# Windowed attention and a mixture of four domains on one core: the bias table is folded earlier, half of the next head pair's q is prepared ahead, and the mask reads SBUF

## The chip, the cores and the metric

The kernel runs on one core of a Trainium2 chip. The metric is device microseconds of one execution, the median of the runs; smaller is better. TensorE (PE in the profile) multiplies matrices, VectorE (DVE), ScalarE (ACT) and GpSimd (POOL) work on elements, SyncE (SP) and ACT issue the transfers of this kernel. Matmuls write to PSUM, which is handed out in banks; all else lies in SBUF.

## The reference

Two parts in a row. First attention in a window, with a bias that grows with the distance between query and key, by a slope for each head:

```
B, H, S, D = 4, 8, 768, 64;  n_global, n_local = 8, 96
scores = q @ k.T / sqrt(D)
rel = pos[:, None] - pos[None, :]
is_global = pos[None, :] < n_global
is_local = (rel >= 0) & (rel < n_local)
dist = where(is_global & ~is_local, n_local, abs(rel))
scores = where(is_global | is_local, scores - slopes[:, None, None] * dist, -1e9)
a = softmax(scores);  x = (a @ v) as [B * S, H * D] = [3072, 512]
```

Then a mixture of E = 4 domains with F = 1024 hidden columns, weighted by the normalised probabilities p of each row:

```
out = sum over e of p[:, e:e+1] * (relu(x @ w1[e]) @ w2[e])
```

## The kernel before

The mixture's products are the bulk of the work. Each float32 operand is split into a rounded high part and a rest, so that a product takes three matmuls (high·high, high·rest, rest·high). The product with w1 is built block by block from seven products of sums of blocks in place of eight (`first`; blocks are called B11, T1 and so on, their epilogues write p, u, vv and h), the one with w2 follows in `second`, and DVE adds it to `acc` by domain.

The kernel runs in three stages. Until about 62 us `attention_early` computes batch 0's attention alone, in the order of the program, with steps that a counter n numbers; `chores` (loads and splits of weights) are woven between, and the step `opening` starts the mixture. Then come batches 0 and 1 of the mixture, one `first` or `second` after the other, each in steps. Between the steps the generator `attention_chain` is advanced, which does the attention of batches 1, 3 and 2, four pairs of heads each, twelve pairs: `count` steps of it over the length `span`. In this stage (from step 14 on, `HELDSTEPS`) the tile scheduler, not the program, sets the order on each engine: it puts an instruction where its model finds it ready, and hands out PSUM slots as they come free. From about 650 us on `late_batch` runs batches 3 and 2 of the mixture with no attention beside.

A pair takes twelve steps before. Three prepare it: half 0 of q (`prepare_q`: three transposes by TensorE into a bank of the pool pt, a scaled copy by ACT and the rest by DVE into qd), half 0 of k (`prepare_k`, the same into kd), half 1 of q. Then six tiles of 128 queries (t = 0 to 5), with one step more before t = 1 (half 1 of k), t = 2 (loads of the next q and k) and t = 3 (`differences` of v). `spread_q` copies qd to the other 64 partitions by transfers that ACT issues, since each head is used with both halves of the partitions. Each step calls `flow`, a pipeline of four tiles: scores of the newest into ps; `softmax` of the next (DVE reads ps and nbias, ACT takes exp into pb with the sum zsum) and the normalising of the one before (ACT scales pb into pn); `turn_folded` transposes pn into a bank of pt and moves it to pT; after the sixth tile `weigh` multiplies pT with v and vg in two halves, each into a bank of pt, which ACT copies to x (batches 1 and 2) or `piece` (batch 3).

A tile sees 96 older keys, its own 128, and 32 global ones. They are folded to 160 columns: an old key and the one that can't be seen at the same place share a column, and `newer` is the mask that tells them apart. For this `nbias`, the table of biases by head, is folded too, and `attention_chain` does so at its first call:

```
ve.tensor_tensor(nbias[:, :, :NPREV], nbias[:, :, :NPREV], nbias[:, :, PL : 2 * P], op=ALU.min)
for to, fro, n in (
    (PL, 2 * P + NGLOB, NPREV), (2 * P + NGLOB, NPREV, NGLOB), (NPREV, P, NGLOB), (P, 2 * P + NGLOB, NGLOB),
):
    ve.tensor_copy(nbias[:, :, to : to + n], nbias[:, :, fro : fro + n])
```

`ve`, `ac`, `po`, `te` and `sy` are the five engines behind a helper; all that goes through it has the helper's line, L43, in the profile, so work is told apart by the names of its tiles.

Of the kernel before, what the change touches and what calls it, by code (L numbers as in the profile page):

```python
# [14 lines left out]
ALU = mybir.AluOpType  # L15
# [3 lines left out]
P = 128  # L19
NEG = 1.0e9  # L20

NGLOB = 32
NPREV = 96
# [163 lines left out]
def attn_moe_kernel(ctx: ExitStack, tc, q, k, v, n_global, n_local, domain_probs, w1, w2, out):  # L187
# [4 lines left out]
    NQT = S // P  # L192
# [246 lines left out]
    def softmax(A, new, old):  # L439


        if old:
            pb, zsum = old["pb"], old["zsum"]
        if new:
            t, pr, ps = new["t"], new["pr"], new["ps"]
            if A.early:
                width = 2 * P
                cols = slice(0, P) if t == 0 else slice(0, width)
                bcol = slice(2 * P, 3 * P) if t == 0 else slice(0, width)
                new["pcol"] = pcol = slice(P, width) if t == 0 else slice(0, width)  # L450
            else:
                width = PL
                cols = slice(NPREV, NPREV + P) if t == 0 else slice(0, width)
                bcol = slice(PL, PL + P) if t == 0 else slice(0, width)
                new["pcol"] = pcol = slice(0, P) if t == 0 else slice(0, width)
                if t:
                    both = new["both"]
                    mask = newer[:, P + NGLOB - NPREV - 1 : P + NGLOB - 1].bitcast(mybir.dt.uint16)
                    ve.copy_predicated(
                        both[:, :, :NPREV], mask[:, None, :].to_broadcast([P, 2, NPREV]), both[:, :, PL:]  # L460
                    )
            nmax = A.small.tile([P, 2], F32, name="nmax")
            new["zsum"] = A.small.tile([P, 2], F32, name="zsum")
            new["pb"] = A.pb.tile([P, 2, width], F32, name="pb")
        for j in range(2):
            if new:
                e = new["pb"][:, j, pcol]
                ve.tensor_tensor_reduce(
                    e, ps[j][:, cols], nbias[:, 2 * pr + j, bcol], 1.0, 3.0e38, ALU.add, ALU.min, nmax[:, j : j + 1]
                )  # L470
                ac.activation(
                    e, e, AF.Exp, bias=nmax[:, j : j + 1], scale=-1.0, accum_out=new["zsum"][:, j : j + 1]
                )
            if old:
                if j == 1:
                    ve.reciprocal(zsum, zsum)
                elif A.early:

                    old["spare"] = spare = A.small.tile([P, 3], F32, name="spare")
                    ve.tensor_scalar(zsum, zsum, 1e-9, None, op0=ALU.add, op1=ALU.add, accum_out=spare[:, 2:3])  # L480
                else:
                    ac.activation(zsum, zsum, AF.Copy, bias=1e-9)
        if old:
            if A.early:
                for j in range(2):
                    p = pb[:, j, old["pcol"]]
                    ve.tensor_scalar(
                        p, p, zsum[:, j : j + 1], None, op0=ALU.mult, op1=ALU.add, accum_out=old["spare"][:, j : j + 1]
                    )
                return  # L490

            old["pn"] = pn = A.pb.tile([P, 2 * PL], F32, name="pn")
            if old["t"]:
                pieces = ((0, pn[:, :PL], pb[:, 0]), (1, pn[:, PL : PL + NGLOB], pb[:, 1, P:]))
            else:
                pieces = ((0, pn[:, :P], pb[:, 0, :P]),)
            for j, dst, src in (*pieces, (1, pn[:, PL + NGLOB :], pb[:, 1, :P])):
                ac.activation(dst, src, AF.Copy, scale=zsum[:, j : j + 1])

    def turn(A, tile_):  # L500
# [11 lines left out]
    def turn_folded(A, tile_):  # L512

        t, pn = tile_["t"], tile_["pn"]
        pt = A.pt.tile([P, 4, P], F32, name="pt")
        pT = tile_["pT"] = A.pT.tile([P, 2, 2, P], F32, name="pT")
        for place, at in enumerate((0, PL + NGLOB, P)[: 3 if t else 2]):
            te.transpose(pt[:, place, :], pn[:, at : at + P], ident)
        if t:
            ve.scalar_tensor_tensor(  # L520
                pT[:NPREV, 0], newer[:NPREV, None, :P].to_broadcast([NPREV, 2, P]), 1.0, pt[:NPREV, :2],
                op0=ALU.subtract, op1=ALU.mult,
            )
            for j in range(2):
                ac.copy(pT[NPREV:, 0, j], pt[j * NGLOB : (j + 1) * NGLOB, 2])
        ac.copy(pT[:, 1], pt[:, :2])

    def weigh(A, three, x, b):

# [25 lines left out]
    def attention_early(A):  # L555
# [66 lines left out]
        while any(tiles):  # L622
            flow()
            yield

    def attention_chain(bs, A):

        tiles, turned = [None] * 4, []
        order = [(b, pr) for b in bs for pr in PAIRS]
        nats, gots = [{} for _ in order], [{} for _ in order]  # L630

        def flow(new=None):

            one, two, three, four = tiles
            if new:
                new["both"] = scores(A, new["t"], gots[new["m"]])
                new["ps"] = [new["both"][:, j] for j in range(2)]
            if four:
                turned.append(four)
            if len(turned) == NQT:  # L640
                b = order[four["m"]][0]
                for half in (turned[:TPH], turned[TPH:]):
                    weigh(A, half, xs[b], b)
                turned.clear()
            if three:
                turn_folded(A, three)
            softmax(A, one, two)
            tiles[:] = [new, one, two, three]

        def fetch_heads(m, names):  # L650
# [6 lines left out]
        po.iota(  # L657
            newer, pattern=[[1, P + NGLOB]], base=1 - NGLOB, channel_multiplier=-1, allow_small_or_imprecise_dtypes=True
        )
        po.tensor_scalar(newer, newer, 0.0, 1.0, op0=ALU.is_gt, op1=ALU.mult)  # L660
        ve.tensor_tensor(nbias[:, :, :NPREV], nbias[:, :, :NPREV], nbias[:, :, PL : 2 * P], op=ALU.min)
        for to, fro, n in (
            (PL, 2 * P + NGLOB, NPREV), (2 * P + NGLOB, NPREV, NGLOB), (NPREV, P, NGLOB), (P, 2 * P + NGLOB, NGLOB),
        ):
            ve.tensor_copy(nbias[:, :, to : to + n], nbias[:, :, fro : fro + n])
        yield
        for m, (b, pr) in enumerate(order):
            if pr == PAIRS[0]:
                xs[b] = None if b == B - 1 else xp.tile([P, NPAIR, S], F32, name="x")
                if b == B - 1:  # L670
                    xd[b] = dp.tile([P, NPAIR, S], F32, name="x_last")
            nat, got = nats[m], gots[m]
            for part, hf in ((prepare_q, 0), (prepare_k, 0), (prepare_q, 1)):
                part(A, nat[part.__name__[-1]], hf, got)
                flow()
                if part is prepare_k:
                    spread_q(0, got)
                yield
            for t in range(NQT):
                if t in (1, 2, 3):  # L680
                    if t == 1:
                        prepare_k(A, nat["k"], 1, got)
                    elif t == 2:
                        fetch_heads(m + 1, "qk")
                    else:
                        nat["vg"] = differences(A, nat["v"])
                    flow()
                    yield
                flow({"t": t, "pr": pr, "m": m, "v": nat})
# [350 lines left out]
    with ExitStack() as start_stack:  # L1040
        A = Pools(start_stack, "start", st=1, kd=2, qd=2, nat=2, natv=3, pb=4, ps=2, pt=3, px=1, early=True)
        for n, _ in enumerate(attention_early(A)):
            if n == 9:
                chores += [load_plain(2), load_w2(0, lead=5, eng=po)]
            if n == 2 * NQT + 5:
                chores += [load_w1(1, lead=2, hold=0, eng=po), first_sums(0)]
            work_chores()
            if n == 4 * NQT + 1:
                opening(A)
        mix = mixture()  # L1050
        next(mix)
    Ordered.on = False
# [470 lines left out]
```

## Time and profile before

| | us |
|---|---|
| median of 3 runs | 1164.09 (1163.98 to 1166.28) |
| the profiled execution | 1165.77 |
| its span, first to last instruction | 1164.0 |
| TensorE busy | 1137.0 |
| DVE busy | 882.2 |
| ACT busy | 630.8 |
| POOL busy | 625.8 |

The span is the time between the first and the last instruction; the profiled execution's own time is 1.77 us longer. Busy time is the union of an engine's instructions. All durations below are from this one execution.

### The profile page before, as it was taken

To read this page: it belongs to the slowest core of one execution; us is meant where nothing else is said; L and a number is where in the kernel's file an instruction comes from. 1 tells how busy PE (TensorE), PEld (TensorE's weight loads), DVE (VectorE), ACT (ScalarE), POOL (GpSimd) and SP (SyncE) were. 2 spreads that over 40 slices of the span, in tenths; PEclk is the share of its full clock that TensorE was granted. 3 is DMA by queue.
4 is the path that set the end of the run, shared out by engine and by line. 5 is a ranking of instruction groups with operands and counts; after the bars stand their busy time and mean duration, and the time that the engine had idled before them with its cause. 6 is when DMAs were issued, how large, how long until landed. Compare 5 with 4: busy or idle time off the path is not lost.

```text
span 1164.0 us, 21323 instructions
## 1 busy us (share of the span) xinstructions
PE 1137.0 (98%) x7414; PEld 1056.0 (91%) x7414; DVE 882.2 (76%) x2069; ACT 630.8 (54%) x1777; POOL 625.8 (54%) x606
## 2 busy tenths in 40 slices
PE   7899999999999999999999999999999999999997
PEld 5678898988898989889898899999999999999997
DVE  7978778777878777787777777777777777777776
ACT  6844777877753665665675334444444444444443
POOL 5667656555453234322222427777778855555554
PEclk9999999999999999999999999999999999999999
DMA  9547989787776888987968668888887687676763
GB/s 183 150 141 277 300 216 305 246 258 198 288 245 227 277 264 264 272 245 241 278 187 277 212 217 301 307 301 301 287 314 280 244 296 249 241 258 227 258 228 132
DMA packets 180978, 290.80 MB, mean 250 GB/s; under 512 B 86784, under 2 KB 137472, under 8 KB 168576
## 3 DMA queue, kind: packets, MB, share of 16 engines
q1 hardware_dynamic: 172992, 273.63, 71.6%
q10 hardware_dynamic: 7872, 15.74, 4.7%
q8 instruction: 61, 1.00, 0.4%
q14 instruction: 53, 0.43, 0.1%
HBM read 207.93 MB, written 70.78 MB: 239 GB/s over the span
## 4 chain that ended last, share of the span: by engine, by line
PE 86%; POOL 4%; DVE 4%; DMA 2%; ACT 2%; issue 2%; ACTq 0%; POOLq 0%; DVEq 0%
PE pm L43 36%; PE pf L43 19%; PE X L43 11%; PE Y L43 9%; PE pt L43 7%; PE ps L43 3%; POOL w1s L43 1%; DMA qd<-qd 1%; DVE pb L43 1%; POOL sums L43 1%; PE px L43 1%; POOL xT L43 1%; POOL xB L43 1%; POOL w2s L43 1%; DMA raw<-in_moe_w_dram 1%
## 5 line engine op out<-in xcount | busy, mean ns | idle before, releaser
L43 PE MATMUL pm<-w2s,h 128*128 128x512 f32 x1152 | 284.6, 396 | 2.6 <-DVE h L43 1.6
L43 PEld LDWEIGHTS pm<-w2s,h 128*128 128x128 f32 x1152 | 210.6, 188 | 45.9 <-DVE h L43 3.8
L43 ACT ACTIVATE hf<-pf 128x384 f32<-128x384 f32 x128 | 62.8, 492 | 248.3 <-DVE pf L43 247.1
L43 POOL TENSOR_TENSOR hS<-sf,hS 128x384 fp32r<-128x384 f32 x126 | 134.2, 1084 | 112.4 <-ACT hS L43 111.6
L43 DVE SCALAR_TENSOR_TENSOR acc<-pm,prob,acc 128x512 f32<-128x512 f32 x180 | 132.6, 747 | 34.1 <-PE pm L43 31.7
L43 PE MATMUL pm<-xT,w1s 128*128 128x384 f32 x744 | 148.7, 341 | 0.0
L43 PE MATMUL pf<-xT,w1s 128*128 128x384 f32 x768 | 146.5, 335 | 0.9 <-ACT hf L43 0.7
L43 POOL TENSOR_TENSOR sums<-raw 128x256 f32<-128x256 f32 x54 | 38.8, 737 | 183.3 <-DMA raw<-in_moe_w_dram 91.2
L43 PEld LDWEIGHTS pf<-xT,w1s 128*128 128x128 f32 x768 | 131.4, 188 | 1.7 <-ACT hf L43 1.2
L43 PEld LDWEIGHTS pm<-xT,w1s 128*128 128x128 f32 x744 | 127.7, 188 | 0.8 <-issue 0.7
L43 DVE TENSOR_TENSOR hA<-hf,hA 128x384 fp32r<-128x384 f32 x94 | 84.6, 926 | 50.6 <-ACT hA L43 50.6
L43 PE MATMUL pm<-xB,w1s 128*128 128x384 f32 x574 | 118.4, 345 | 2.5 <-DVE h L43 2.4
L43 ACT ACTIVATE pb<-pb,nmax 128x160 f32<-128x160 f32 (+2 forms) x192 | 84.4, 447 | 48.9 <-DVE nmax L43 44.6
L43 PE MATMUL pf<-xB,w1s 128*128 128x384 f32 x576 | 110.7, 335 | 0.2 <-ACT hf L43 0.2
L43 PEld LDWEIGHTS pm<-xB,w1s 128*128 128x128 f32 x574 | 99.4, 188 | 8.2 <-DVE h L43 2.8
L43 ACT ACTIVATE h<-pm 128x384 fp32r<-128x384 f32 x128 | 62.2, 491 | 70.0 <-DVE pm L43 66.5
L43 PEld LDWEIGHTS pf<-xB,w1s 128*128 128x128 f32 x576 | 98.7, 188 | 0.5 <-ACT hf L43 0.4
L43 POOL TENSOR_TENSOR sf<-hf 128x384 f32<-128x384 f32 x63 | 70.4, 1117 | 43.6 <-ACT hf L43 43.6
L43 ACT COPY pT<-pt 128x256 f32<-128x256 f32 (+2 forms) x216 | 71.1, 329 | 21.7 <-DVE pT L43 12.7
L43 DVE SCALAR_TENSOR_TENSOR h<-pm,h 128x384 fp32r<-128x384 f32 x128 | 69.6, 551 | 10.6 <-ACT h L43 9.1
L43 PE MATMUL Y<-w2b,hS 128*128 128x256 f32 x576 | 74.0, 282 | 0.0
L43 PE MATMUL X<-w2b,hS 128*128 128x256 f32 x576 | 73.9, 282 | 0.0
(168 smaller groups left out, 2250.7 us busy)
## 6 DMA issues: line engine op xcount, KB each, us to landing
w1s<-kept SPq DMA_DIRECT2D x47, 1792.0 KB, 8.0
w2b<-kept SPq DMA_DIRECT2D x224, 256.0 KB, 4.2
kept<-w1s SPq DMA_DIRECT2D x16, 1792.0 KB, 7.7
raw<-in_moe_w_dram SPq DMA_DIRECT2D x43, 512.0 KB, 5.2
kept<-w2s SPq DMA_DIRECT2D x16, 1024.0 KB, 9.2
w2s<-kept SPq DMA_DIRECT2D x16, 1024.0 KB, 6.2
qd<-qd ACTq DMA_DIRECT2D x48, 192.0 KB, 4.3
q<-in_q_dram SPq DMA_DIRECT2D x30, 192.0 KB, 5.1
```

The lines of the kernel that those rows point to most:

```text
L43: ins = fn(*args, **kwargs)
```

## The change

It has four parts. The fold of nbias and the making of `newer` become a function, `fold_biases`, called in step 26 of the first attention, the one after `opening`. It has three copies in place of four, on POOL, because the first tile of a sequence (t = 0) now reads its own keys and their biases in their natural order; in exchange its pn is put together from four pieces. In `turn_folded` the masked product comes after ACT's copy and reads that copy in SBUF, not the bank of PSUM. A pair takes eleven steps: half 0 of q is prepared ahead of the fifth tile (t = 4) of the pair before, the extra step before t = 2 loads this pair's v, the one before t = 3 goes, `differences` comes after t = 4, and the next q and k are loaded after t = 1 and t = 3. `count` follows, 138 for 149 steps.

```diff
@@ softmax
-                cols = slice(NPREV, NPREV + P) if t == 0 else slice(0, width)
-                bcol = slice(PL, PL + P) if t == 0 else slice(0, width)
+                cols = slice(2 * NGLOB, 2 * NGLOB + P) if t == 0 else slice(0, width)
+                bcol = slice(2 * P, 3 * P) if t == 0 else slice(0, width)
...
             else:
-                pieces = ((0, pn[:, :P], pb[:, 0, :P]),)
-            for j, dst, src in (*pieces, (1, pn[:, PL + NGLOB :], pb[:, 1, :P])):
+                pieces = [
+                    (j, pn[:, j * (PL + NGLOB) + to : j * (PL + NGLOB) + to + n], pb[:, j, fro : fro + n])
+                    for j in range(2) for to, fro, n in ((0, NGLOB, NPREV), (NPREV, 0, NGLOB))
+                ]
+            for j, dst, src in pieces:
                 ac.activation(dst, src, AF.Copy, scale=zsum[:, j : j + 1])
@@ turn_folded
         if t:
-            ve.scalar_tensor_tensor(
-                pT[:NPREV, 0], newer[:NPREV, None, :P].to_broadcast([NPREV, 2, P]), 1.0, pt[:NPREV, :2],
-                op0=ALU.subtract, op1=ALU.mult,
-            )
             for j in range(2):
                 ac.copy(pT[NPREV:, 0, j], pt[j * NGLOB : (j + 1) * NGLOB, 2])
         ac.copy(pT[:, 1], pt[:, :2])
+        if t:
+            ve.scalar_tensor_tensor(
+                pT[:NPREV, 0], newer[:NPREV, None, :P].to_broadcast([NPREV, 2, P]), 1.0, pT[:NPREV, 1],
+                op0=ALU.subtract, op1=ALU.mult,
+            )
@@ new function, called at n == 4 * NQT + 2
+    def fold_biases():
+        po.iota(
+            newer, pattern=[[1, P + NGLOB]], base=1 - NGLOB, channel_multiplier=-1, allow_small_or_imprecise_dtypes=True
+        )
+        po.tensor_scalar(newer, newer, 0.0, 1.0, op0=ALU.is_gt, op1=ALU.mult)
+        ve.tensor_tensor(nbias[:, :, :NPREV], nbias[:, :, :NPREV], nbias[:, :, PL : 2 * P], op=ALU.min)
+        for to, fro in ((PL, NPREV), (NPREV, P), (P, PL)):
+            po.tensor_copy(nbias[:, :, to : to + NGLOB], nbias[:, :, fro : fro + NGLOB])
@@ attention_chain
-            for part, hf in ((prepare_q, 0), (prepare_k, 0), (prepare_q, 1)):
+            for part, hf in ((prepare_k, 0), (prepare_q, 1)):
...
             for t in range(NQT):
-                if t in (1, 2, 3):
-                    if t == 1:
-                        prepare_k(A, nat["k"], 1, got)
-                    elif t == 2:
-                        fetch_heads(m + 1, "qk")
-                    else:
-                        nat["vg"] = differences(A, nat["v"])
+                if t == 1:
+                    prepare_k(A, nat["k"], 1, got)
+                if t == 4 and m + 1 < len(order):
+                    prepare_q(A, nats[m + 1]["q"], 0, gots[m + 1])
+                if t in (1, 2, 4):
                     flow()
+                    if t == 2 and m:
+                        fetch_heads(m, "v")
                     yield
                 flow({"t": t, "pr": pr, "m": m, "v": nat})
                 if t == 0:
                     spread_q(1, got)
-                if t == 0 and m:
-                    fetch_heads(m, "v")
+                elif t == 1:
+                    fetch_heads(m + 1, "q")
+                elif t == 3:
+                    fetch_heads(m + 1, "k")
+                elif t == 4:
+                    if m + 1 < len(order):
+                        spread_q(0, gots[m + 1])
+                    nat["vg"] = differences(A, nat["v"])
                 yield
@@ the loop over the mixture's steps
-    count, span = 3 * NPAIR * (6 + NQT) + 5, (LATE * 13 * per - 12) * 0.97
+    count, span = 3 * NPAIR * (5 + NQT) + 6, (LATE * 13 * per - 12) * 0.97
```

How the instructions move is shown at three places. The first is DVE in the first steps of the mixture, where one product's epilogue writes u, vv, pm and h. Before, the fold stands among them:

```order
L43 TENSOR_TENSOR u<-pm,p_1187 128x384
L43 TENSOR_TENSOR nbias<-nbias 128x8x96
L43 TENSOR_TENSOR vv<-pm,u 128x384
L43 COPY nbias<-nbias 128x8x96
L43 COPY nbias<-nbias 128x8x32
L43 TENSOR_TENSOR u<-pm,u 128x384
L43 COPY nbias<-nbias 128x8x32
L43 TENSOR_TENSOR pm<-pm,vv 128x384
L43 COPY nbias<-nbias 128x8x32
L43 TENSOR_TENSOR pm<-pm,p_1187 128x384
L43 SCALAR_TENSOR_TENSOR h<-pm,h 128x384
```

Of the change, on the same engine at the same product:

```order
L43 TENSOR_TENSOR u<-pm,p_1193 128x384
L43 TENSOR_TENSOR vv<-pm,u 128x384
L43 TENSOR_TENSOR u<-pm,u 128x384
L43 TENSOR_TENSOR pm<-pm,vv 128x384
L43 TENSOR_TENSOR pm<-pm,p_1193 128x384
L43 SCALAR_TENSOR_TENSOR h<-pm,h 128x384
```

The fold's copies stand on POOL now, between the split of the first units' w1 (w1s) and that of w2 (w2s), at the end of the first attention:

```order
L43 CAST w1s<-sums 128x512
L43 TENSOR_TENSOR w1s<-sums,w1s 128x512
L43 IOTA newer 128x160
L43 TENSOR_SCALAR newer<-newer 128x160
L43 COPY nbias<-nbias 128x8x32 x3
L43 CAST w2s<-raw_1057 128x512
```

So five instructions leave DVE's epilogues, and five, the mask's two among them, come ahead of a split on POOL; the minimum on DVE moves to the same step.

The second place is TensorE where the tenth pair is weighed, ahead of the eleventh pair's half 1 of k: matmuls with v and vg are the weighing (the first half is ten of them, the second twelve), those with ident are transposes, pm is a product of the mixture. Before, from the first half's last four on:

```order
L43 MATMUL pt<-pT,v 64x128 x2
L43 MATMUL pt<-pT,vg 64x128 x2
L43 MATMUL pt<-pT,v 64x128 x2
L43 MATMUL pt<-pT,vg 64x128 x2
L43 MATMUL pt<-pT,v 64x128 x2
L43 MATMUL pt<-pT,vg 64x128 x2
L43 MATMUL pt<-pT,v 64x128 x2
L43 MATMUL pt<-pT,vg 64x128 x2
L43 MATMUL pm<-xB_4563,w1s 128x384 x6
L43 MATMUL pm<-xT_4625,w1s 128x384 x6
L43 MATMUL pt<-ident,k 128x128 x3
```

Of the change, from the transposes of k on; the second half begins behind the five matmuls on xB_4569, and its first matmul waits there for ACT:

```order
L43 MATMUL pt<-ident,k 128x128 x3
L43 MATMUL pt<-pT,v 64x128 x4
L43 MATMUL pt<-pT,vg 64x128 x2
L43 MATMUL pt<-pT,v 64x128 x2
L43 MATMUL pt<-pT,vg 64x128 x2
L43 MATMUL pm<-xB_4569,w1s 128x384 x5
L43 MATMUL pt<-pT,v 64x128 x2
L43 MATMUL pt<-pT,vg 64x128 x2
L43 MATMUL pt<-pT,v 64x128 x2
L43 MATMUL pt<-pT,vg 64x128 x2
L43 MATMUL pt<-pT,v 64x128 x2
L43 MATMUL pt<-pT,vg 64x128 x2
```

The transposes of k, which came two products behind the weighing, come just ahead of it, and five matmuls of a product stand between its halves. ACT at the same place, before:

```order
L43 COPY x<-pt 128x384 x2
L43 ACTIVATE pb,zsum<-pb,nmax 128x128 x2
L43 ACTIVATE zsum<-zsum 128x2
L43 ACTIVATE h<-pm 128x384
L43 ACTIVATE pn<-pb,zsum 128x128 x2
L43 CAST kd<-pt 64x3x128
L43 ACTIVATE h<-pm 128x384
L43 CAST kd<-pt 64x3x128
```

And of the change:

```order
L43 CAST kd<-pt 64x3x128
L43 ACTIVATE h<-pm 128x384 x2
L43 CAST kd<-pt 64x3x128
L43 COPY x<-pt 128x384
L43 ACTIVATE pn<-pb,zsum 128x96
L43 ACTIVATE pn<-pb,zsum 128x32
L43 ACTIVATE pn<-pb,zsum 128x96
L43 ACTIVATE pn<-pb,zsum 128x32
L43 COPY x<-pt 128x384
```

The copy of the first half, which led, now stands behind two casts for kd and two of h. In 11 of the 12 pairs the weighing is split like this: in six of them with a product's matmuls on xB in the gap, in five with four or five matmuls against w2s there and, on ACT, a cast of weights or an exp in the place of the two h.

The third place is TensorE ahead of a pair's first tile. Before, from the transposes of half 0 of q:

```order
L43 MATMUL pt<-ident,q 128x128 x3
L43 MATMUL pt<-ident,pn 128x128 x3
L43 MATMUL pm<-w2s,h 128x512 x12
L43 MATMUL pt<-ident,k 128x128 x3
L43 MATMUL pm<-xB_4561,w1s 128x384 x2
L43 MATMUL pt<-ident,pn 128x128
L43 MATMUL pm<-xB_4561,w1s 128x384 x2
L43 MATMUL pt<-ident,pn 128x128 x2
L43 MATMUL pm<-xB_4561,w1s 128x384 x2
L43 MATMUL pm<-xT_4579,w1s 128x384 x6
L43 MATMUL pm<-xT_4591,w1s 128x384 x2
```

Of the change:

```order
L43 MATMUL pt<-ident,q 128x128 x3
L43 MATMUL pm<-xB_4619,w1s 128x384 x6
L43 MATMUL pm<-xB_4569,w1s 128x384 x6
L43 MATMUL ps<-kd,qd 128x256 x4
L43 MATMUL pt<-ident,pn 128x128 x3
L43 MATMUL pm<-xT_4631,w1s 128x384 x6
L43 MATMUL pm<-w2s,h 128x512 x6
L43 MATMUL ps<-kd,qd 128x256 x4
L43 MATMUL pt<-ident,pn 128x128 x3
L43 MATMUL pm<-w2s,h 128x512 x18
L43 MATMUL pt<-ident,k 128x128 x3
L43 MATMUL pm<-w2s,h 128x512 x12
```

The pair's first scores follow 36 matmuls of the mixture behind the transposes of q before, and 66 behind them in the change: the two tiles of scores shown still belong to the pair before. Behind the transposes of k there are 24 of them in both.

## Rows read from the trace of the kernel before

**Rows 1.** The page's busy time of each engine.
```profile
PE 1137.0 (98%) x7414; PEld 1056.0 (91%) x7414; DVE 882.2 (76%) x2069; ACT 630.8 (54%) x1777; POOL 625.8 (54%) x606
```

**Rows 2.** Busy time by stage (the columns are named in the first line).
```profile
core 0: us, PE busy (x) PEld busy (x) DVE busy (x) ACT busy (x) POOL busy (x), PEclk, DMA share, GB/s
...
62.00:100.00 38.00, 34.33 (x156) 27.74 (x157) 33.15 (x58) 16.74 (x32) 32.42 (x29) 1.00 0.64 208
100.00:650.00 550.00, 544.13 (x3343) 490.52 (x3342) 427.32 (x1071) 355.87 (x1101) 229.85 (x221) 1.00 0.80 252
```

**Rows 3.** TensorE's waits, 62 to 100 us: in total, times, longest.
```profile
PE pm L43 <- DVE h L43: 3.1, 2, 2.4
```

**Rows 4.** DVE's timeline at 82 to 91 us: start, duration, work.
```profile
82.97 1.12 DVE L43 TENSOR_TENSOR nbias<-nbias 128x768 bf16<-128x768 bf16 x1
...
84.48 2.21 DVE L43 COPY nbias<-nbias 128x768 bf16<-128x768 bf16 x2
...
87.08 0.28 DVE L43 COPY nbias<-nbias 128x256 bf16<-128x256 bf16 x1
...
87.75 1.29 DVE L43 COPY nbias<-nbias 128x256 bf16<-128x256 bf16 x1
```

**Rows 5.** TensorE's timeline there; in brackets the wait before.
```profile
90.03 1.15 PE L43 MATMUL pm<-xB,w1s 128*128 128x384 f32 x5 [2.43 <-DVE h L43]
```

**Rows 6.** POOL's timeline, 56 to 68 us.
```profile
67.08 1.86 POOL L43 TENSOR_TENSOR xT<-xB,xT 128x768 fp32r<-128x768 f32 x1 [11.05 <-ACT xT L43]
```

**Rows 7.** DVE's timeline, 57.5 to 63 us.
```profile
62.28 0.56 DVE L43 TENSOR_TENSOR xB<-x 128x384 f32<-128x384 f32 x1 [4.78 <-ACT x L43]
```

**Rows 8.** TensorE's waits, 100 to 650 us, the first four lines.
```profile
PE ps L43 <- DMA qd<-qd: 1.6, 2, 1.2
PE pt L43 <- ACT pn L43: 1.3, 1, 1.3
PE pm L43 <- DVE h L43: 1.0, 2, 0.6
PE pt L43 <- ACT pT L43: 0.8, 1, 0.8
```

**Rows 9.** TensorE's timeline around one wait for qd, and qd's transfers.
```profile
512.75 0.49 PE L43 MATMUL pt<-ident,q 128*128 128x128 f32 x3
...
523.46 0.50 PE L43 MATMUL ps<-kd,qd 128*128 128x256 f32 x2 [1.19 <-DMA qd<-qd]
...
DMA to landing us min/median/max: 2.5/4.3/8.2
```

**Rows 10.** Timelines of ACT and TensorE at the first pair's first pn.
```profile
123.38 0.69 ACT L43 ACTIVATE pn<-pb,zsum 128x128 f32<-128x128 f32 x2
124.77 0.62 ACT L43 CAST w1s<-sums 128x512 fp32r<-128x512 f32 x1 [0.70 <-POOL sums L43]
...
123.83 0.62 PE L43 MATMUL pt<-ident,pn 128*128 128x128 f32 x2 [1.26 <-ACT pn L43]
124.20 1.64 PE L43 MATMUL pm<-w2s,h 128*128 128x512 f32 x6
```

**Rows 11.** Timelines of TensorE and ACT at one weighing.
```profile
524.59 0.66 PE L43 MATMUL pt<-pT,v 128*64 128x128 f32 x8
...
527.14 1.68 PE L43 MATMUL pm<-xB,w1s 128*128 128x384 f32 x8
528.66 0.49 PE L43 MATMUL pt<-ident,k 128*128 128x128 f32 x3
...
529.18 0.47 ACT L43 CAST kd<-pt 64x384 fp32r<-64x384 f32 x1 [0.20 <-PE pt L43]
529.56 0.48 ACT L43 ACTIVATE h<-pm 128x384 fp32r<-128x384 f32 x1
```

**Rows 12.** DVE's groups by form, 100 to 650 us, and the page's group of hA.
```profile
L43 DVE SCALAR_TENSOR_TENSOR pT<-newer,pt 96x256 f32<-96x256 bf16 x60 | 24.6, 410 | 5.4 <-PE pt L43 5.3
...
L43 DVE TENSOR_TENSOR pm<-pm,vv 128x384 f32<-128x384 f32 x56 | 31.3, 558 | 6.5 <-PE pm L43 6.5
...
L43 DVE TENSOR_TENSOR hA<-hf,hA 128x384 fp32r<-128x384 f32 x94 | 84.6, 926 | 50.6 <-ACT hA L43 50.6
```

More of the change, by code (lines that the diff above doesn't have):

```diff
@@ L493, in softmax @@
             if old["t"]:
-                pieces = ((0, pn[:, :PL], pb[:, 0]), (1, pn[:, PL : PL + NGLOB], pb[:, 1, P:]))
-            else:
-                pieces = ((0, pn[:, :P], pb[:, 0, :P]),)
-            for j, dst, src in (*pieces, (1, pn[:, PL + NGLOB :], pb[:, 1, :P])):
+                pieces = (
+                    (0, pn[:, :PL], pb[:, 0]), (1, pn[:, PL : PL + NGLOB], pb[:, 1, P:]),
+                    (1, pn[:, PL + NGLOB :], pb[:, 1, :P]),
+                )
+            else:
+                pieces = [
[3 more added lines that the diff above has]
+            for j, dst, src in pieces:
                 ac.activation(dst, src, AF.Copy, scale=zsum[:, j : j + 1])
@@ L624, in attention_early @@
             yield
+    def fold_biases():
+        po.iota(
+            newer, pattern=[[1, P + NGLOB]], base=1 - NGLOB, channel_multiplier=-1, allow_small_or_imprecise_dtypes=True
+        )
+        po.tensor_scalar(newer, newer, 0.0, 1.0, op0=ALU.is_gt, op1=ALU.mult)
+        ve.tensor_tensor(nbias[:, :, :NPREV], nbias[:, :, :NPREV], nbias[:, :, PL : 2 * P], op=ALU.min)
+        for to, fro in ((PL, NPREV), (NPREV, P), (P, PL)):
+            po.tensor_copy(nbias[:, :, to : to + NGLOB], nbias[:, :, fro : fro + NGLOB])
     def attention_chain(bs, A):
@@ L656, in attention_chain @@
         fetch_heads(0, "qkv")
[L657 to L665, printed above, removed]
         yield
+        prepare_q(A, nats[0]["q"], 0, gots[0])
+        flow()
+        yield
+        spread_q(0, gots[0])
         for m, (b, pr) in enumerate(order):
@@ L672, in attention_chain @@
             nat, got = nats[m], gots[m]
-            for part, hf in ((prepare_q, 0), (prepare_k, 0), (prepare_q, 1)):
+            for part, hf in ((prepare_k, 0), (prepare_q, 1)):
                 part(A, nat[part.__name__[-1]], hf, got)
                 flow()
-                if part is prepare_k:
-                    spread_q(0, got)
                 yield
             for t in range(NQT):
-                if t in (1, 2, 3):
-                    if t == 1:
-                        prepare_k(A, nat["k"], 1, got)
-                    elif t == 2:
-                        fetch_heads(m + 1, "qk")
-                    else:
-                        nat["vg"] = differences(A, nat["v"])
+                if t == 1:
[3 more added lines that the diff above has]
+                if t in (1, 2, 4):
                     flow()
+                    if t == 2 and m:
+                        fetch_heads(m, "v")
                     yield
@@ L1049, in attn_moe_kernel @@
                 opening(A)
+            if n == 4 * NQT + 2:
+                fold_biases()
         mix = mixture()
```

## The prediction

> **What bounds the kernel now.** I read four views, from coarse to fine. The page's list of busy times comes first [rows 1]: TensorE is busy 1137.0 of 1164.0 us, so 27 us is all that any reordering can win. The table of busy times by stage [rows 2] says where the part lies that this change can reach: 3.67 us in 62 to 100 us (the mixture's first steps, no attention yet), and 5.87 us in 100 to 650 us (twelve head pairs woven into the mixture). The granted clock is 1.00 in both, so a microsecond of wait removed is one won. Then I read TensorE's waits in the two stages, for what each waits on [rows 3, 8], and followed the large ones into the timelines. The reader should see that of the 3.67 us 2.43 is a single stop [rows 5], and that of the 5.87 us 4.7 are six waits of at most 1.3 us [rows 8]. TensorE's own work does not change: the same matmuls and transposes are issued.
>
> **The fold of the biases.** Before, DVE runs one minimum and four copies on nbias among the epilogues of a product: 1.12 + 2.21 + 0.28 + 1.29 = 4.90 us [rows 4]. TensorE stops right behind them, 2.43 us at 90.03, for DVE's h [rows 5]. Taking 4.90 us out of a queue that was 2.43 us late leaves some 2.4 us to spare: −2.43. The other 0.7 us of waits for h in that stage (3.1 less 2.4, [rows 3]) has another place and stays.
> What is added lies at the end of the first attention. POOL gets three copies of 8x32 columns beside the mask's two instructions, which are shorter than such a copy (160 columns for 256). No row has this copy on POOL; DVE's rows of it bound it, 0.28 and 1.29 us [rows 4]. So POOL needs 1.4 to 6.5 us. It stands idle for the 11.05 us before 67.08 [rows 6], from 56.03 on, so it is done by 62.5 and the instruction at 67.08, which waits for ACT, does not move. DVE's minimum, 1.12 us, falls in the 4.78 us idle before 62.28 [rows 7]. I cost both at nothing; without that cover the first product would start up to 1.1 us later for DVE, and up to 6.5 for POOL.
> The other order of keys for t = 0 gives ACT four pieces of pn for two, 24 more instructions over twelve pairs, at no more than 0.35 us each (0.69 for two, [rows 10]): 8 us at most. ACT has 194 us idle of 550 [rows 2], so this matters only where TensorE waits for pn.
>
> **The first pn.** There is one such place: TensorE waits 1.26 us at 123.83 [rows 10]. In the new order of ACT the same pn stands behind the cast that starts at 124.77, and in four pieces; TensorE comes there six products against w2s later, about 1.4 us (the row of six, 1.64 with its overlap, [rows 10]). If that cast stays where it is, pn starts at 125.3 and its four pieces end at 126.7; TensorE, idle from 122.57, would arrive at 123.97 and wait 2.7 us: +1.5. If the casts come earlier, because the load of weights on which they hang no longer shares its queue with loads of k just then, the wait vanishes: −1.3. I take +0.5, nearer the upper end, because the order on ACT is certain and the earlier load is not.
>
> **Half of the next q ahead of the fifth tile.** Two waits of TensorE for qd, 1.6 us, are the largest item in 100 to 650 [rows 8]; one is the 1.19 us at 523.46 [rows 9]. The copy of qd to the other 64 partitions is a transfer that ACT issues, and it needs 2.5 to 8.2 us to land [rows 9]. Before, 9.5 us lie between the transposes of q, 512.75, and the start of that wait, 522.27. Now sixty-six matmuls of the mixture stand between them: thirty of 0.19 us (eight in 1.52 us from 527.14 to 528.66, [rows 11]) and thirty-six of 0.23 (six in 1.4), 14 us without the attention's own. That is 4.5 us or more of room against 1.2 missing: −1.6 in all. To pay would be k, whose load is now issued after t = 3, not t = 2; its transposes stand where they stood against the scores, and TensorE shows no wait for a load of k in the list that [rows 8] begins, though how near it was no row says. I take 0, with a bound of 1 for two pairs late by 0.5, as qd is now.
> Fewer steps (138 for 149) over the same length keep two units of the mixture per pair, so the stages end where they did.
>
> **The weighing of v is split.** A pair's six tiles are weighed in two halves, each into a PSUM bank of pt. Before, the halves stand together. Now, in 11 of the 12 pairs, k's second half is transposed just ahead, four or five products come between the halves, and the second half waits for ACT. The bound, counted from the start of the transposes: in six places ACT must do kd, h, h, kd and the copy of the first half. At 0.47 to 0.48 each [rows 11] behind 0.49 us of transposes that is 2.88 us. TensorE comes to the second half after the transposes (half of the 0.49, since the next work starts before their modelled end), ten of the 22 matmuls that take 2.55 us from 524.59 to 527.14 [rows 11], 1.16, and five products, 0.95: 2.35 us. Missing: 0.53 at each of six places, and by the same count with a cast in the place of h up to 0.2 at each of five, 4.2 us in all. The lower bound is 0: ACT's instructions start 0.38 us apart for 0.47 of length (529.18 and 529.56, [rows 11]), or h is done before. The nearest rows for such a meeting of TensorE and ACT are two waits in [rows 8]: of 72 tiles' pn and 12 weighings, put in their places by the same scheduler, one each was late, by 1.3 and by 0.8. They speak for the lower end, the count for the upper; I take +1.0.
>
> **The mask reads SBUF.** Sixty instructions on DVE of 410 ns [rows 12] read ACT's copy in place of PSUM. They begin one ACT copy later, and the PSUM bank comes free by ACT alone. TensorE's list has one wait for the finished pT, 0.8 us [rows 8], so this chain has room nearly everywhere. The price of the new instruction stands in no row: with one operand in PSUM an addition of 128x384 takes 558 ns, with both in SBUF 926 on average in this kernel [rows 12]. At that ratio 410 becomes 680, and sixty add 16 us to a DVE with 123 us idle of 550 [rows 2]. Bounds: 0 to 16 us on DVE, on TensorE only where DVE is late already; I take 0.
> The Trainium skill, page "SBUF — State Buffer", section "Who interferes with whom", says that a DVE instruction with two SBUF inputs contends with a GpSimd instruction that reads SBUF, one blocking the other for its whole length, and that one with at most one SBUF input does not. The 926 against 558 ns agree with it. By that rule the sum would be that of the third rival, +1.5 for the −2.5 below.
>
> **The sum.** −2.43 − 1.6 + 0.5 + 1.0 = −2.5 us. The profiled execution took 1165.77 us, 1.77 of it outside the span, and would take 1163.2; it lies 1.68 over the median of the three runs, 1164.09, so the median becomes **1161.6 us**. This case alone reaches from 1160.1 (first pn and halves at 0) to 1163.6 (+1.5 and +2.0). What a measurement can't tell from no change is within 0.2%, 1161.8 to 1166.4; the forecast stands on its edge.
>
> **The rivals.**
> *The second halves are late (slower).* Each of 11 places waits 0.6 us: six by the count above, the others if ACT is 0.4 us later, as behind one more cast. 6.6 − 2.43 − 1.6 + 0.5 = +3.1, 1167.2 us. It decides the sign from 0.32 us a place (3.5 over 11), and the time is slower beyond 0.2% from 0.53. For it: in six places a kd that stands behind two h is on the way. Against it: how rare such waits are in [rows 8].
> *The time won early is given back.* The stop at 90.03 goes, but TensorE reaches the next work that hangs on loads of weights 2.4 us earlier and waits there, for instance at the first pn: −1.6 + 1.0 = −0.6, 1163.5 us. For it: ACT waits there for POOL's sums, 0.70 us at 124.77 [rows 10]. Against it: only this one wait of the kind stands in [rows 8].
> *The mask in SBUF slows DVE.* Of the 16 us at the ratio of [rows 12] a quarter reaches the products' epilogues, whose h is waited for twice already [rows 8]: +4.0 − 2.5, 1165.6 us. Against it: POOL is busy 230 of 550 us here [rows 2], so most of the sixty would meet an idle POOL.
> *All short waits go.* DVE is freed of 4.9 us and banks of pt come free earlier; the 5.87 us in 100 to 650 fall to 2: −2.43 − 3.9, 1157.8 us, with the halves at their lower bound.
> *The move of q does nothing.* The stop at 523.46 passes to kd: −0.9, 1163.2 us, in the forecast's own range.
>
> **How the numbers follow.** Forecast 0.46, the last rival included (0.27 of it faster, 0.19 the same); late halves 0.22 (slower 0.17, same 0.05); given back 0.13 (faster 0.03, same 0.10); DVE slowed 0.07 (same 0.04, slower 0.03); all short waits gone 0.12 (faster). So faster 0.42, same 0.38, slower 0.20. The range reaches from the fourth rival to the first, 1157.8 to 1167.2; each end cuts through its case, which leaves about 2 in 10 outside.
>
> **What would show it.** In the new trace: no stop of TensorE near 88 to 90 us and no nbias on DVE from 82 to 88; no wait of ps for qd in 100 to 650; near 122 to 127 a wait for pn of 0 to 2.7 us; at the second halves waits of pt for ACT's x or piece of 0.1 us each, 0.6 if the first rival holds; the mask's instruction at 410 ns, nearer 680 if the third does. The forecast is wrong if a wait that no row names (a load of k or v, a bank of ps) comes up, or if TensorE's 1137.0 us change.

## The result and the profile after

The changed kernel takes 1172.06 us (median of 6 runs, 1169.71 to 1173.2), the kernel before 1165.07 in the runs beside them: a ratio of 1.0057, interval 1.0043 to 1.0072. It is some 6.6 us slower; the forecast was 2.5 us faster, with 1167.2 as the upper end. The profiled execution took 1172.39 us with a span of 1170.6.

The profile after, read in the order in which that of before was read. Busy time of each engine, from the page, and then by stage (the columns as in [rows 2]):

```profile
PE 1141.7 (98%) x7414; PEld 1054.6 (90%) x7414; DVE 887.0 (76%) x2065; ACT 635.9 (54%) x1801; POOL 628.8 (54%) x609
```
```profile
62.00:100.00 38.00, 37.07 (x169) 30.27 (x170) 30.57 (x55) 16.61 (x31) 31.00 (x27) 1.00 0.67 223
100.00:650.00 550.00, 539.82 (x3265) 480.72 (x3264) 428.77 (x1061) 358.31 (x1119) 225.13 (x215) 1.00 0.78 251
```

Beside [rows 2], TensorE is busy 2.7 us more in 62 to 100: the first stage gave what was forecast. From 100 to 650 it idles 10.2 us instead of 5.9. And with the same 7414 matmuls its busy time is 4.7 us longer than in [rows 1], which the prediction had named as a sign that it is wrong.

TensorE's waits in 100 to 650 (total, times, longest), to be held against [rows 8]:

```profile
PE pt L43 <- ACT pn L43: 3.5, 3, 3.2
PE pt L43 <- ACT x L43: 2.0, 3, 0.7
PE pm L43 <- DVE h L43: 1.5, 3, 0.8
PE pt L43 <- DVE kd L43: 1.0, 2, 0.7
PE pm L43 <- DVE acc L43: 0.7, 1, 0.7
PE pt L43 <- ACT piece L43: 0.7, 1, 0.7
```

The waits for qd are gone. The first pn holds TensorE 3.2 us, and the lines with x and piece are the second halves of the weighing: four waits of 0.7 us each.

A list of waits leaves out what lies under the modelled end of the matmul before. So I also took the start of each matmul from both traces and formed the intervals to the next one, from the place of the stop near 88 us to the end of the attention. For each pair of neighbours (a matmul of one kind followed by one of another) the lowest tenth of its intervals is called the usual one, and the table counts what lies above it, in us. That stretch is 6.8 us longer after the change:

| where | before, us over the usual | after |
|---|---|---|
| the stop at 88 to 90 | 2.6 | 0 |
| between matmuls of ps (qd) | 2.7 | 0.6 |
| the first pn, both its transposes | 1.6 | 3.7 |
| the other transposes of pn | 1.2 | 4.0 |
| into and inside the weighing, from another matmul | 1.5 | 3.5 |
| from a product on w1 to w2, and from ps to w2 | 0.7 | 2.3 |

The usual intervals themselves add 1.9 us, since a weighing in two parts is entered and left twice (11 times some 0.17 us). The rest, some 1.1 us, is spread over the products in steps of at most 0.15 us.

### The profile page after: what moved, and what is told of

Its sections match the earlier page's. It is cut to its first block, busy times and chain, and to the rows that moved or that the text cites. A ratio compares the mean times of both kernels' runs of the same rounds, so it can differ in the third digit from the quotient of the medians.

```text
span 1170.6 us, 21402 instructions
## 1 busy us (share of the span) xinstructions
PE 1141.7 (98%) x7414; PEld 1054.6 (90%) x7414; DVE 887.0 (76%) x2065; ACT 635.9 (54%) x1801; POOL 628.8 (54%) x609
## 4 chain that ended last, share of the span: by engine, by line
PE 80%; DVE 7%; ACT 6%; POOL 3%; issue 2%; DMA 2%; ACTq 0%; SPq 0%; DVEq 0%; POOLq 0%
PE pm L43 32%; PE pf L43 19%; PE X L43 11%; PE Y L43 9%; PE pt L43 5%; PE ps L43 3%; ACT pb L43 1%; POOL w1s L43 1%; DVE pb L43 1%; DMA raw<-in_moe_w_dram 1%; ACT pT L43 1%; POOL w2s L43 1%; DVE qd L43 1%; DVE pT L43 1%; POOL sums L43 1%
## 5 line engine op out<-in xcount | busy, mean ns | idle before, releaser
L43 ACT ACTIVATE pn<-pb,zsum 128x32 f32<-128x32 f32 (+3 forms) x228 | 71.1, 368 | 17.6 <-DVE zsum L43 16.6
```

The lines of the kernel that those rows point to most:

```text
L43: ins = fn(*args, **kwargs)
```

## The experiments

Each run has the kernel before beside it on the same chip; ratios are to that.

**The parts one by one.** fold_only is the kernel before with `fold_biases`, its call, the natural key order and pn in four pieces:

```diff
-        ve.tensor_tensor(nbias[:, :, :NPREV], ...)     # at the first call of attention_chain
-        ve.tensor_copy(...)                            # four copies
+            if n == 4 * NQT + 2:
+                fold_biases()
```

> The kernel before with the fold alone: fold_biases at the first attention's end, t = 0 in natural key order with pn in four pieces. Theory (the order of the eleven-step pair costs the time; the fold itself gains what was forecast): no nbias on DVE at 82 to 88 us and no stop of TensorE at 88 to 90, the first pn waits as before or up to 0.5 us longer, so 1.5 to 2.6 us faster than before. Rival (the four pieces of pn cost it): a longer wait at the first pn and small waits at t = 0 of each pair, no gain or slower.

Measured: 1163.39 us, 0.9978 (0.9969 to 0.9987). As the theory had it: 2.2 us at the medians. The work that was added costs little. POOL's five instructions take 2.2 us, near the lower end of the prediction's 1.4 to 6.5 (the second of the mask's two takes 0.77 us, longer than a copy, where the prediction had it shorter), and DVE's minimum takes half of the 1.12 us before. These are the groups of nbias on POOL and DVE in the changed kernel (min, median, max in ns):

```profile
L43 POOL COPY nbias<-nbias x3: 396/400/400, 57.8 to 58.7; 128x256 bf16<-128x256 bf16 x3
L43 DVE TENSOR_TENSOR nbias<-nbias x1: 552/552/552, 57.1 to 57.1; 128x768 bf16<-128x768 bf16 x1
```

In fold_only the first pn waits 1.3 us, as in [rows 8], so the four pieces cost nothing that the list of waits shows.

pair_only is the kernel before with the new loop of `attention_chain` and its `count`:

```diff
-            for part, hf in ((prepare_q, 0), (prepare_k, 0), (prepare_q, 1)):
+            for part, hf in ((prepare_k, 0), (prepare_q, 1)):
...
+                if t == 4 and m + 1 < len(order):
+                    prepare_q(A, nats[m + 1]["q"], 0, gots[m + 1])
```

> The kernel before with the eleven-step pair and its count alone; fold at the chain's first call and mask on PSUM as before. Theory (order): slower than before by 4 to 9 us, with the waits for ACT at the weighing's second halves, a first pn wait near 3 us, and the weighings split on TensorE; no wait for qd. Rival (the mask in SBUF makes DVE late, and the order alone is harmless): between 2 us faster and 1 us slower than before.

Measured: 1169.64 us, 1.0034 (1.0021 to 1.0047), so 4.0 us slower, the lower edge of what the theory said. But the waits for ACT's x and piece at the second halves, on which the theory rested, are not there: the waits over 0.5 us in 100 to 650 are the first pn (2.3) and one on acc (0.8). The weighings are split here too, 11 of the 12, but the transposes of k stand right ahead of only 6.

mask_only is the kernel before with the new `turn_folded`:

```diff
-                ..., 1.0, pt[:NPREV, :2],       # ahead of ACT's copies
+                ..., 1.0, pT[:NPREV, 1],        # behind them
```

> The kernel before with the masked product alone moved behind ACT's copy and reading it in SBUF. Theory (order): the sixty products get longer, by some 5 to 8 us in all, as in the changed kernel, but the weighings stay whole and DVE's delay is hidden: within 1.5 us of before. Rival (the mask is the cause): 3 us slower or more, with waits of TensorE for h or pn that were not there.

Measured: 1176.46 us, 1.0092 (1.0079 to 1.0105). The theory falls: the mask alone, with whole weighings, costs 10.8 us, more than the whole change. Its waits in 100 to 650:

```profile
PE pt L43 <- ACT pT L43: 4.1, 4, 1.2
PE ps L43 <- DMA qd<-qd: 3.9, 2, 3.6
PE pt L43 <- ACT pn L43: 2.0, 4, 1.3
PE pm L43 <- DVE h L43: 1.7, 3, 1.0
```

weigh_first is the changed kernel with the weighing ahead of k's second half:

```diff
-                if t == 1:
-                    prepare_k(A, nat["k"], 1, got)
...
                     flow()
+                    if t == 1:
+                        prepare_k(A, nat["k"], 1, got)
```

> The changed kernel with one edit: in the step ahead of t = 1 the flow (with the weighing) comes ahead of half 1 of k, not behind it. Theory (order): both halves stand together again, so the waits at the second halves (3.0 us) and the extra openings and closings on TensorE (1.9 us) go: 3 to 5 us faster than the changed kernel, near 1168. Rival (mask): DVE is as late as before and the time moves to other waits, within 1.5 us of the changed kernel.

Measured: 1163.08 us, 0.9984 (0.9973 to 0.9995): 9 us faster than the changed kernel, nearly twice what the theory said, with all twelve weighings whole and no wait at a second half. So neither part alone explains the loss: moving the mask costs 10.8 us in the old order, and with the new order and whole weighings the kernel is no slower than before. What I took from this, to be tested, was that the mask makes DVE late, and that the order decides whether TensorE feels it.

**How the mask makes DVE late.** DVE's group of the product in the changed kernel, 100 to 650 us (busy, mean ns; then idle before it):

```profile
L43 DVE SCALAR_TENSOR_TENSOR pT<-newer,pT 96x256 f32<-96x256 bf16 x60 | 32.2, 537 | 7.2 <-ACT pT L43 6.1
```

[rows 12] has 24.6 us and 410 ns for it. The mean hides the point: the median is 422 ns, and fifteen of the sixty take 505 to 1350. One place where TensorE waits, the weighing at 488 us, on POOL, DVE, ACT and TensorE in turn:

```profile
485.79 2.39 POOL L43 TENSOR_TENSOR sums<-sums,raw 128x1024 fp32r<-128x1024 f32 x1
...
487.12 1.34 DVE L43 SCALAR_TENSOR_TENSOR pT<-newer,pT 96x256 f32<-96x256 bf16 x1
488.39 0.55 DVE L43 TENSOR_TENSOR pm<-pm,vv 128x384 f32<-128x384 f32 x1
488.86 0.55 DVE L43 TENSOR_TENSOR pm<-pm,p 128x384 f32<-128x384 f32 x1
...
488.02 0.47 ACT L43 CAST kd<-pt 64x384 fp32r<-64x384 f32 x1 [0.52 <-PE pt L43]
488.97 0.96 ACT L43 ACTIVATE h<-pm 128x384 fp32r<-128x384 f32 x2 [0.48 <-DVE pm L43]
489.95 0.47 ACT L43 CAST kd<-pt 64x384 fp32r<-64x384 f32 x1
490.45 0.48 ACT L43 COPY piece<-pt 128x384 f32<-128x384 f32 x1
...
489.15 1.14 PE L43 MATMUL pm<-xB,w1s 128*128 128x384 f32 x5
490.98 0.44 PE L43 MATMUL pt<-pT,v 128*64 128x128 f32 x4 [0.69 <-ACT piece L43]
```

POOL's subtraction runs until 488.18; the product on DVE, begun at 487.12, ends at 488.46, 0.28 us behind it. Of the sixty, 25 begin while an instruction of POOL runs, 42%, about POOL's share of the stage (225 of 550 us); all 25 end 0.28 to 0.34 us behind the end of that instruction, however long it still had to run, and the other 35 take 0.41 to 0.42 us. In mask_only it is the same with 24 of sixty (0.28 to 0.39 us behind). With the operand in PSUM none is held: in the kernel before, 27 of the sixty begin while an instruction of POOL runs, and the longest of all takes 0.42 us. Behind the product stand DVE's two sums into pm, on them ACT's two h, behind these kd and the copy of the first half, and on that copy TensorE's second half. At this place the order of the change passes a delay of 0.9 us on DVE through to TensorE.

no_sub tests this chain without touching the order: it leaves out one instruction of POOL, and the instructions of TensorE, DVE and ACT stand in the order of the changed kernel.

```diff
-        po.tensor_tensor(low.bitcast(F32R), low, high, op=ALU.subtract)
```

> The changed kernel without one instruction of GpSimd in each load of the late domains' w2, the subtraction over 128x1024 of 2.39 us that splits the sums (left out, so the low parts hold the whole sums); the order of the matmuls is the same. Theory A (the mask's product, with both operands in SBUF, stands still while GpSimd reads SBUF, and DVE is late for h): the four mask instructions of 1.34 us at 487, 528, 570 and 611 us fall to 0.42, the four waits of 0.75 us at the second halves fall to 0.2 to 0.4, 1.5 to 3 us faster than the changed kernel. Theory B (ACT's order alone makes the second half late): the four waits stay over 0.6, less than 0.7 us of change.

Measured: 1170.21 us, 1.0035 (1.0023 to 1.0047), 1.9 us under the changed kernel at the medians. At the same place of the profile, DVE and TensorE:

```profile
486.95 0.41 DVE L43 SCALAR_TENSOR_TENSOR pT<-newer,pT 96x256 f32<-96x256 bf16 x1
```
```profile
490.15 0.44 PE L43 MATMUL pt<-pT,v 128*64 128x128 f32 x4
```

The product takes 0.41 us, and TensorE does not wait; the same holds at the three later places. One weighing earlier it is the other way round. In no_sub the product there begins under a cast of POOL, and the second half of that weighing waits:

```profile
445.54 1.27 DVE L43 SCALAR_TENSOR_TENSOR pT<-newer,pT 96x256 f32<-96x256 bf16 x1
```
```profile
449.33 0.44 PE L43 MATMUL pt<-pT,v 128*64 128x128 f32 x4 [0.60 <-ACT piece L43]
```

In the changed kernel that product takes 0.52 us and TensorE does not wait. So the wait comes and goes with the hold at the same order of instructions, and theory A holds: these waits come from DVE being held by POOL, not from ACT's order by itself. The time gained is less than the 3.0 us of the four waits: the one at 449 us is new, and the first pn waits 0.5 us longer in this profile.

The operand alone, in both orders. mask_late_psum is the kernel before, late_psum the changed kernel, each with the product behind ACT's copies and reading PSUM:

```diff
-                ..., 1.0, pT[:NPREV, 1],
+                ..., 1.0, pt[:NPREV, :2],
```

> The kernel before with the masked product behind ACT's copies, as in the change, but still reading PSUM; beside mask_only (10.8 us slower than before) it differs in the operand alone, though the scheduler may place neighbours differently. Theory A (two operands in SBUF let GpSimd hold DVE): all sixty products stay at 410 ns and the time is within 3 us of before. Rival (the place behind ACT's copies, and the order that the scheduler makes of it, is the cause): 8 us slower or more, as mask_only.

> The changed kernel with the masked product where the change puts it, but reading PSUM. Theory A (operand in SBUF): as fold_pair, 4 to 5 us faster than the changed kernel, near 1167 to 1168, with no wait of 0.7 us at the second halves. Rival (the place and the order): within 1.5 us of the changed kernel, 1170.5 to 1173.5.

Measured: mask_late_psum 1167.04 us, 1.0018 (1.0008 to 1.0027), where mask_only had 1.0092; late_psum 1166.07 us, 1.0011 (1.0000 to 1.0021), where the changed kernel had 1.0057. Theory A in both. The groups of the product in mask_only and then in mask_late_psum (min, median, max):

```profile
L43 DVE SCALAR_TENSOR_TENSOR pT<-newer,pT x60: 412/422/1379, 131.5 to 654.2; 96x256 f32<-96x256 bf16 x60
```
```profile
L43 DVE SCALAR_TENSOR_TENSOR pT<-newer,pt x60: 404/417/419, 131.9 to 644.4; 96x256 f32<-96x256 bf16 x60
```

By the ratios, reading SBUF costs 8.6 us of the 10.8 in the old order and 5.4 of the 6.6 in the new one. The scheduler places some neighbours differently with either operand (the transposes of k stand right ahead of the weighing in 6 pairs of late_psum, in 11 of the changed kernel). So these figures hold the operand together with the order that it brings about; the waits that no_sub removed at equal order are the part shown to be the hold alone.

fold_pair is the changed kernel with `turn_folded` as before.

> The changed kernel with the mask as before (reading PSUM, ahead of ACT's copies). If the parts added up it would be 1.8 us slower than the kernel before (minus 2.2 for the fold, plus 4.0 for the pair). Theory A (the mask's new place costs time in either order of the pair): 1.5 to 3 us slower than before, so 4 to 5 us faster than the changed kernel, with the waits at the second halves small. Theory B (the split of the weighing costs nearly all): as slow as the changed kernel, 5 us or more over before.

Measured: 1167.33 us, 1.0008 (0.9999 to 1.0017), 1.4 us over the kernel before at the medians, near the sum of fold_only and pair_only, and no wait for x or piece in 100 to 650. Theory A.

**The first pn.** wf_pool is weigh_first, with the casts of one load of w1 on POOL:

```diff
-                    chores.append(load_w2(i + 2, wait=wait) if fn is second else load_w1(i + 2, wait))
+                    chores.append(load_w2(i + 2, wait=wait) if fn is second else
+                                  load_w1(i + 2, wait, eng=po if (fn, i) == (first, 3) else ac))
```

> weigh_first (half 1 of k behind the flow), and the casts of the one load of w1 that stands ahead of the first pn on ACT are given to GpSimd. Theory (the first pn waits because ACT stands in that cast, behind a transfer): the wait of 2.3 us at about 121 us goes or falls under 0.5, 1.8 to 2.8 us faster than weigh_first, near 1161. Rival (something behind it is as late: the normalisation or GpSimd, now busier): under 0.8 us of gain.

Measured: 1161.04 us, 0.9954 (0.9941 to 0.9968). Its waits in 100 to 650:

```profile
PE pm L43 <- DVE h L43: 1.7, 4, 0.8
PE pt L43 <- DVE kd L43: 1.2, 1, 1.2
PE pm L43 <- DVE acc L43: 0.7, 1, 0.7
```

The wait of 2.3 us for pn is gone, and there is a new one of 1.2 us at 145 us, on kd, behind DVE. The theory holds: 2.0 us faster than weigh_first at the medians. At the medians this is 4.9 us faster than the kernel before, and 11 us faster than the change as it was made, with two edits.

**What is left of the mask.** weigh_first_psum and wf_pool_psum are weigh_first and wf_pool with `turn_folded` as before:

> weigh_first with the mask as before (reading PSUM, ahead of ACT's copies). Theory A (the mask in SBUF costs DVE 8 us of which some reaches TensorE): 1 to 4 us faster than weigh_first. Theory B (with whole weighings DVE's delay is hidden; the scheduler now splits five weighings): within 1 us of weigh_first, or slower by up to 2.

> wf_pool with the mask as before. With whole weighings the mask in SBUF cost less than the five weighings that the scheduler splits without it (weigh_first_psum was 2.1 us slower than weigh_first). If that holds here: 1 to 3 us slower than wf_pool, near 1163. If the 2.1 us came from the first pn's neighbourhood alone, which wf_pool has mended: within 0.7 us of wf_pool.

Measured: 1165.21 us, 0.9989 (0.9979 to 1.0000), and 1161.38 us, 0.9965 (0.9954 to 0.9977). The intervals overlap those of weigh_first and wf_pool, so no difference can be told, in either direction (at the medians they are 2.1 and 0.3 us slower): theory B of the first, the second outcome of the other. This does not show that the hold is free with whole weighings. Reading PSUM, the scheduler splits five of the twelve weighings in both kernels, with six matmuls against w2s in the gap, so the operand is again compared together with an order, and a loss on one side can hide one on the other.

wf_pool_sub4 cuts POOL's long subtraction:

```diff
-        po.tensor_tensor(low.bitcast(F32R), low, high, op=ALU.subtract)
+        for n in range(4):
+            po.tensor_tensor(low[:, n].bitcast(F32R), low[:, n], high[:, n], op=ALU.subtract)
```

> wf_pool with GpSimd's subtraction over 128x1024 (2.39 us) cut into four of 128x256. If a long instruction of GpSimd holds DVE for its whole rest, the longest of the sixty products fall from 1.35 to 0.8 us; TensorE waits at none of them any more, so 0 to 1 us faster than wf_pool, 1160 to 1161.5. Slower than 1162 would say that the cut costs GpSimd, or the loads behind it, more than it frees.

Measured: 1160.55 us, 0.9963 (0.9951 to 0.9974), the same as wf_pool within the intervals; the longest of the sixty products took 1.18 us, for 1.35 in wf_pool. Less than expected, since POOL has other instructions of a microsecond.

## Why the prediction was wrong

**The step that failed** is "on TensorE only where DVE is late already; I take 0" for the mask. It had both halves of the answer: the ratio of 926 to 558 ns in [rows 12], and the section "Who interferes with whom" of the Trainium skill, page "SBUF — State Buffer", which says that a DVE instruction with two SBUF inputs contends with a GpSimd instruction that reads SBUF, and that the order of issue decides which of the two is blocked. The trace agrees with it to the end times (0.28 to 0.39 us behind POOL's end, in all 49 cases of the changed kernel and mask_only). The two mistakes were in what was made of it. I took a mean for the price of each instruction, 270 ns more for every one of the sixty. The group's spread in the trace of the kernel before shows that no such price was paid by each (min, median, max):

```profile
L43 DVE TENSOR_TENSOR hA<-hf,hA x94: 557/806/1372, 691.0 to 1144.5; 128x384 fp32r<-128x384 f32 x94
```

The shortest takes 557 ns, as much as the addition with an operand in PSUM. Seventeen of the 94 take 557 to 559 ns; the other 77 begin while an instruction of POOL runs and end 0.41 to 0.42 us behind its end. So the 926 was the hold already, averaged over a stage with other work on POOL, and the mean was too high here (the sixty took 7.7 us more, not 16). But the hold comes as fifteen delays of 0.1 to 0.9 us, and the four that TensorE was seen to wait for are the longest. And I asked only whether DVE has idle time (123 us of 550), not which instruction stands behind the product: it is the sum into pm, and on that hang h, kd and the bank for which TensorE waits. The third rival was the right one, and got 0.07. Its +4.0 us came near the 5.4 measured in part by luck: it is a quarter of 16 us where 7.7 came, and the 5.4 holds the scheduler's order as well.

**The weighing.** The bound worked out from ACT's queue was 0.53 us a place at six places; TensorE waited 0.7 at four of them. Without the hold (no_sub) it waited at none of the four, so my "0 if h is done before" was the truth of the order by itself, and the 1.0 that I took, for 2.0 in the table, stood for the wrong cause. The sign of the first rival, waits of 0.6 at the second halves, came at these four of its eleven places, for the same other reason. What the sum lacked altogether is that a weighing in two parts is entered and left twice: 1.9 us on an engine whose "own work does not change".

**The first pn**: +0.5 was taken, with +1.5 as the bound; it was +2.1. The mechanism is as told: pn behind the cast of w1s in ACT's queue, the cast behind POOL's sums, these behind a load. ACT and TensorE in the changed kernel, to be held against [rows 10]:

```profile
122.79 0.62 ACT L43 CAST w1s<-sums 128x512 fp32r<-128x512 f32 x1 [0.90 <-POOL sums L43]
...
123.74 1.07 ACT L43 ACTIVATE pn<-pb,zsum 128x96 f32<-128x96 f32 x4 [0.23 <-DVE zsum L43]
...
124.38 0.33 PE L43 MATMUL pt<-ident,pn 128*128 128x128 f32 x1 [3.17 <-ACT pn L43]
```

pn starts 0.36 us later than before, far less than the bound had it, since the load did land earlier. But TensorE comes there at 121.2, not at 123.97: the 2.6 us won at 88 us bring it to a load that has not moved as far. This is the second rival, at the place that it named; it took most of what the fold had given in the changed kernel (2.1 of 2.6), and fold_only, where pn stands ahead of that cast, kept it.

**The fold and the move of q** were right. The stop at 90 us went, −2.6 for −2.43, and fold_only shows 2.2 us of it in the time. The waits for qd went, −2.1 for −1.6, though the transfers take longer to land than in [rows 9]:

```profile
DMA to landing us min/median/max: 2.5/6.2/10.6
```

**Other small waits.** 2.8 us more at the remaining transposes of pn and 1.6 at the entries into w2 came from nothing the prediction named. The same count of intervals in the other traces divides them. At the transposes of pn, pair_only and fold_pair, whose product reads PSUM, have 3.2 us and late_psum 2.2, for 1.2 before and 4.0 in the changed kernel: a good part comes with the new order of the pair. At the entries into w2 those three have 0.9 to 1.0 us, for 0.7 before; every run in the new order whose product reads SBUF (weigh_first, no_sub and wf_pool too) has 2.1 to 2.3, so most of that goes with the operand and the order it brings; which of the two, the runs don't say.

## What to carry to other kernels

Before moving an operand of VectorE from PSUM to SBUF, look at what GpSimd runs beside it: price the longest hold, not the mean, and follow it down the queue to the next engine that waits for a bank. Count an instruction group that is split as entered and left twice, even where its work is the same. Time won ahead of a load is kept only if the queue that stands behind the load does not hold the next thing that the bottleneck needs: here four casts moved off ACT were worth about as much as the fold (2.0 and 2.2 us at the medians).

## What the runs showed of the hardware

Beside the hold, the granted clock of TensorE falls to half, 1.2 GHz, for 3.4 us at a time, at places that differ from run to run. Nine of the fourteen profiles have one such stretch at 48 to 55 us. From there to the last microseconds of the program there are nine more, in eight profiles, and each begins at or less than 2 us behind the end of a stop of TensorE. The fourteen profiles have twelve stops of 2.2 to 3.7 us in that part, so nine of the twelve have such a stretch. weigh_first, at its first pn (the third column from the end is the clock):

```profile
121.40:124.90 3.50, 3.32 (x11) 3.03 (x12) 0.00 (x0) 2.73 (x11) 3.21 (x3) 0.52 1.12 360
```

and pair_only, behind the stop that the fold removes:

```profile
89.50:92.90 3.40, 3.40 (x13) 3.40 (x12) 1.45 (x3) 1.59 (x4) 3.18 (x6) 0.50 0.97 310
```

The changed kernel's own profile has the stop at 121 us and no such stretch behind it, and the kernel before has none behind its stop at 88, so a stop does not always bring one. By these lengths half the clock for 3.4 us is worth up to 1.7 us, an estimate; that is about half of the distance between the runs of one kernel (1163.1 to 1166.3 before). The four profiles without such a stop (fold_only, wf_pool, wf_pool_psum, wf_pool_sub4) have none that begins between 55 us and those last microseconds. Whether a stop removed gives that time back as well stays open: from weigh_first to wf_pool, where a wait of 2.3 us goes and one of 1.2 comes, it is 2.0 us by the medians and 3.5 by the ratios.
